# Bias as a ninth summand of the logits, a tile's factors in a tile of their own, and the next slot's gathers and scaling ahead of the scatters

## The chip, the cores and the metric

The kernel runs on one core of a Trainium2 chip. The metric is the device time of one execution in microseconds (us), the median over runs. TensorE is the matmul engine, VectorE (DVE) and ScalarE (ACT) the two engines that also read matmul results out of PSUM, GpSimd (POOL) the fourth, which here also issues the indirect DMAs; SyncE (SP) issues the other DMAs.

## What is computed

Attention over keys and values that are averaged over groups of 8 positions, then a mixture of experts in which each token goes to the one expert with the largest logit. Sizes: q, k, v are 8 x 8 x 576 x 64; 4608 tokens of width 512; 8 experts with a hidden width of 1024; 2 modalities.

```python
k_p = k.reshape(B, H, Sp, 8, D).mean(axis=3)            # v_p likewise
scores = scale * q @ k_p^T;  scores -= max;  attn = exp(scores) / (sum + 1e-9)
x = (attn @ v_p) as [4608, 512]
logits = x @ w_gate + modality_bias[modality_id]
e_idx = argmax(logits);  gate_w = softmax(logits)[e_idx]
out[tokens of e] = gate_w * (relu(x @ w1[e]) @ w2[e])
```

## The kernel before

**Attention.** 36 tiles of 128 tokens, in 20 steps (`steps`, L462); a step holds one or two tiles (z = 0 and 1), and a step with one tile mixes two batches. The loop at L906 works on a step in pieces that follow the engines' names: `s_pe`/`s_dve`/`s_act` make scores, subtract their maximum (`mx` L540, `sb` L543) and exponentiate; `t_pe`/`t_act` transpose the result (`pt`, L567); `a_pe` (L583) multiplies it by the values into one PSUM accumulator `av`, of which there is a single buffer. The values carry two more column groups: each head's product with the gate weights, and a column of ones, so that `av` also holds each head's eight logit shares and its sum. Pooling of k and v for the next batches runs on POOL (`fold`, L302 to L306), hooked into certain steps; in step 5 a hook also builds `bias_all`, the modality bias of all tokens, on POOL (`modality_terms`, L446).

**`x_dve(t)` (L603)** takes a tile out of `av`: DVE forms the sums (`s8`, L620), their reciprocals `r` (L622), and multiplies the logit shares by them into `lgs[g]` (L624), a tile for the nine token tiles of a group. For tiles with `late` (groups 2 and 3, z = 1; eight of them) the reciprocal is written into the row buffer `xw` itself, at its columns RX, and ACT copies the unscaled output beside it (L627); those rows are scaled after they are gathered again. For the others DVE multiplies the output by the factors (L630, `xb`). Rows go to the DRAM buffer `xs` by SP.

**`route(g)` (L661)** is a list of small DVE operations: reduction over the 8 heads (L679), bias add (L680), maximum over experts (L681), difference and exponential (L684, ACT L685), mask of the largest (L688), and so on. For groups 0 to 2 the list goes into `drip`; `gap(n)` takes up to n operations off its head at fixed places between the operations of `s_dve` and `x_dve`. Of the list of group 3, seven operations are issued at the end of the attention (L983) and the others, by their numbers in the list, inside the first expert slots (L1102).

**Experts.** Tokens sorted by expert are worked in slots of 256 rows (`part(s)`, L1124; 18 slots in this data, `NSTAT` = 18). Weights are split in two float32r halves by ACT and DVE; a slot is 8 times 12 matmuls `hp` (L170) and 6 matmuls `op` (L1160), and the 8 transposes (L161) of the next slot's rows. In a slot s, at f = 0, the previous slot's result is scaled by the gates (`evac`, L1131: DVE L1136, ACT L1138) and scattered by two indirect DMAs (L1142); then POOL gathers the next slot's rows with two indirect DMAs (L1204 by way of L143), scales them by the factors at f = 3 (L1219 by way of L152), and TensorE transposes them at f = 5. `evac(later=...)` puts the scatters into a list that is emptied behind the scaling; before, only slot 1 uses it. All engines execute their instructions in program order; the order above is written out by hand.

Of the kernel before, what the change touches and what calls it, by code (L numbers as in the profile page):

```python
# [9 lines left out]
F32 = mybir.dt.float32  # L10
# [12 lines left out]
P = 128  # L23
SLOT = 256
EARLY_GROUPS = 2
EARLY_SLOTS = 2
# [4 lines left out]
def kernel(  # L31
# [12 lines left out]
    nc = tc.nc  # L44
    ctx.enter_context(tc.manual_schedule(engines=ENGINES))
    B, H, S, HD = q.shape
    NTOK, D = out.shape
    E, _, FF = w1.shape
# [9 lines left out]
    RX = D + 8  # L58
    NSTAT = NTOK // SLOT
    NSLOT = (NTOK + EARLY_SLOTS * SLOT - 1 - E) // SLOT + E  # L60
    NCOL = 2 * NSLOT
    GT = 9
    GROUPS = [(GT * i, GT) for i in range(B // 2)]
# [127 lines left out]
    with ExitStack() as actx:  # L191
        ap = actx.enter_context(tc.tile_pool(name="ap", bufs=1))
# [207 lines left out]
        bias_all = ap.tile([P, NT, E], F32, name="bias_all")  # L400
# [182 lines left out]
        def a_pe(t):  # L583
# [9 lines left out]
            for u in range(2):  # L593
# [6 lines left out]
                for hs, y in halves:  # L600
                    nc.tensor.matmul(dst4[hs], pt4[:, hs], v4[y][:, 2 * u:2 * u + 2, :], start=False, stop=True)  # L601

        def x_dve(t):  # L603
            n, z = tile_step[t]
            g, gi = tile_group[t]
            av = avs.pop(t)
            mixed = steps[n][1] is None
            b = steps[n][0]
            if gi == 0:
                lgs[g] = late_p.tile([P, GT, H, E], F32, tag="lg", bufs=2, name=f"lg_{g}")  # L610
            xw = xbs[n if n < NX0 else NX0 + n % (len(xbs) - NX0)]
            xo = xw[:, z, 0:D]
            avv = av[:, :, 0:4 * VC].rearrange("p u (h x) -> p u h x", h=4)
            s8 = ap.tile([P, 2, 4], F32, tag="r", bufs=4, name=f"r_{t}")


            late = g >= EARLY_GROUPS and z == 1
            r = xw[:, z, RX:RX + H].rearrange("p (u h) -> p u h", u=2) if late else s8
            rb = r.rearrange("p u (h o) -> p u h o", o=1)
            nc.vector.tensor_scalar(s8, avv[:, :, :, VC - 1], float(POOL), 1e-9 * POOL, op0=ALU.mult, op1=ALU.add)  # L620
            gap(1)
            nc.vector.reciprocal(r, s8)  # L622
            gap(1)
            nc.vector.tensor_tensor(lgs[g][:, gi].rearrange("p (u h) e -> p u h e", u=2), avv[:, :, :, HD:HD + E],  # L624
                                    rb.to_broadcast([P, 2, 4, E]), op=ALU.mult)
            if late:
                nc.scalar.copy(xo.rearrange("p (u h d) -> p u h d", u=2, h=4), avv[:, :, :, 0:HD])  # L627
            else:
                for u in range(2):
                    nc.vector.tensor_tensor(xo[:, u * D // 2:(u + 1) * D // 2].rearrange("p (h d) -> p h d", h=4),  # L630
                                            avv[:, u, :, 0:HD], rb[:, u].to_broadcast([P, 4, HD]), op=ALU.mult)
            gap(2)

            if mixed:
                for y in range(2):
                    r0 = (b - 1 + y) * S + 512
                    stores.append(lambda y=y, r0=r0: nc.sync.dma_start(xs[r0:r0 + 64, :], xw[64 * y:64 * y + 64, 0, :]))
            elif z == 1:
                jj = steps[n][1]
                stores.append(lambda: nc.sync.dma_start(  # L640
                    xs[b * S:b * S + 512, :].rearrange("(p j) x -> p j x", j=4)[:, 2 * jj:2 * jj + 2, :], xw))
# [19 lines left out]
        def route(g):  # L661

            t0, n = GROUPS[g]
            sl = slice(t0, t0 + n)
            lg = small("lgr", g, [P, n, E])
            ex = small("ex", g, [P, n, E])
            m1 = small("m1", g, [P, n])
            m2 = small("m2", g, [P, n])
            sm = small("sm", g, [P, n])
            dc = small("dc", g, [P, E])  # L670
            rs = small("rs", g, [P, n, E])
            rk = small("rk", g, [P, n])
            rki = small("rki", g, [P, n], I32)
            rkm = small("rkm", g, [P, n], I32)
            rkf = small("rkf", g, [P, n])
            V = nc.vector
            ops = []
            add = ops.append
            add(lambda: V.reduce_sum(lg, lgs[g].rearrange("p t h e -> p t e h"), axis=AX.X))  # L679
            add(lambda: V.tensor_add(lg, lg, bias_all[:, sl, :]))  # L680
            add(lambda: V.reduce_max(m1, lg, axis=AX.X))  # L681

            def sub():
                V.tensor_tensor(lg, lg, per_e(m1, n), op=ALU.subtract)  # L684
                nc.scalar.activation(ex, lg, AF.Exp)  # L685
            add(sub)

            add(lambda: V.scalar_tensor_tensor(lg, lg, 0.0, per_t(w8, n), op0=ALU.is_equal, op1=ALU.mult))  # L688
            add(lambda: V.reduce_max(m2, lg, axis=AX.X))
            add(lambda: V.tensor_tensor(oh[:, sl, :], per_t(w8, n), per_e(m2, n), op=ALU.is_equal))  # L690

            def pe():
                if g == len(GROUPS) - 1:
                    pr = ps_tr.tile([P, n, E], F32, tag="tr", name=f"pr_{g}")
                else:
                    pr = corner(n * E).rearrange("p (t e) -> p t e", e=E)
                nc.tensor.matmul(pr, tri, oh[:, sl, :], start=True, stop=False)
                nc.tensor.matmul(pr, ones, cum[:, g:g + 1, :].to_broadcast([P, n, E]), start=False, stop=False)
                for i in range(n - 1):
                    m = n - 1 - i  # L700
                    nc.tensor.matmul(pr[:, i + 1:n, :], ones, oh[:, t0 + i:t0 + i + 1, :].to_broadcast([P, m, E]),
                                     start=False, stop=(i == n - 2))
                rts[g] = pr
                if g == 0:
                    rts["e0"] = corner(E, n * E)
                    nc.tensor.matmul(rts["e0"], sel0, oh[:, 0, :], start=True, stop=True)
            add(lambda: V.reduce_sum(sm, ex, axis=AX.X))
            add(lambda: V.tensor_scalar_add(sm, sm, 1e-9))
            add(lambda: V.reduce_sum(dc, oh[:, sl, :].rearrange("p t e -> p e t"), axis=AX.X))

            def gates():
                V.reciprocal(gate[:, sl], sm)
                for z in range(2):
                    b = 2 * g + z
                    nc.sync.dma_start(xs[b * S:b * S + 512, D:D + 1].rearrange("(p j) o -> p (j o)", j=4),
                                      gate[:, t0 + 5 * z:t0 + 5 * z + 4], allow_slow_non_contiguous=True)
                    nc.sync.dma_start(xs[b * S + 512:(b + 1) * S, D:D + 1],
                                      gate[64 * z:64 * z + 64, t0 + 4:t0 + 5], allow_slow_non_contiguous=True)
            add(gates)
            add(lambda: V.tensor_add(cum[:, g + 1, :], cum[:, g, :], dc))  # L720
            held.add(pe)
            add(pe)
            if g == 0:
                add(lambda: V.tensor_copy(e0oh, rts["e0"]))
            if g >= EARLY_GROUPS:
                add(lambda: V.tensor_tensor(rs, rts[g], per_t(adjv, n), op=ALU.add))
                add(lambda: V.tensor_mul(rs, rs, oh[:, sl, :]))
            else:
                add(lambda: V.tensor_tensor(rs, rts[g], oh[:, sl, :], op=ALU.mult))
            add(lambda: V.reduce_sum(rk, rs, axis=AX.X))  # L730
            add(lambda: V.tensor_copy(rki, rk))
            add(lambda: V.tensor_single_scalar(rkm, rki, 127, op=ALU.bitwise_and))
            add(lambda: V.tensor_single_scalar(rki, rki, 7, op=ALU.logical_shift_right))
            add(lambda: V.tensor_copy(rkf, rkm))
            add(lambda: V.tensor_copy(rh[:, sl], rki))
            for i in range(n):
                add(lambda i=i: V.tensor_scalar(arow[:, t0 + i, :], iota_b, rkf[:, i:i + 1], None, op0=ALU.is_equal))
            return ops
# [70 lines left out]
        def at(hook, n, *fns):  # L809
            hook.setdefault(n, []).extend(fns)  # L810
# [38 lines left out]
        for f in range(NF):  # L849
            at((hook_1, hook_2, hook_3)[(f + 1) % 3], N - 2 + (f + 1) // 3, lambda f=f: first0(f))  # L850

        at(hook_0, 5, modality_terms)

        load_gate()
        load_k(1)
# [124 lines left out]
            gap()  # L980
        loads(N + 1)
        last_route = route(len(GROUPS) - 1)
        for fn in last_route[:7]:  # L983
            fn()


# [110 lines left out]
    ]  # L1097


    lr, c4 = last_route, 2 * EARLY_SLOTS  # L1100
    first_cols = table(c4, c4 + 6)
    late = {  # L1102
        (0, 0): [lr[9], lr[7], lr[11], lr[8]],
# [20 lines left out]
    def part(s):  # L1124
# [68 lines left out]
        def run(fs, tail):  # L1193
            later = []
            for f in fs:
                if f:
                    hidden(f)
                if f == 0:
                    if s == 1:
                        tail(later=later)  # L1200
                    else:
                        tail()
                    if nxt and EARLY_SLOTS <= s < NSTAT - 1:
                        gather(s + 1, gidx, 2 * (s + 1), xg)  # L1204
# [130 lines left out]
```

## Time and profile before

| | |
|---|---|
| median of 3 runs | 625.12 us (623.38 to 627.63) |
| the profiled execution | 627.34 us, span 625.5 us |
| TensorE matmuls busy | 601.5 us (96% of the span) |
| DVE / ACT / POOL busy | 414.8 / 347.6 / 245.8 us |
| mean granted TensorE clock | 0.996 of full speed |
| last matmuls of the attention | about 187 us |

A busy TensorE is not one at its peak, since matmuls overlap and their ends are modelled; what counts for an edit is where TensorE waits, and for whom. Times in rows are from the start of the span.

### The profile page before, as it was taken

What the parts mean: (1) busy time and instruction counts of PE and PEld (TensorE: products, weight loads), DVE (VectorE), ACT (ScalarE), POOL (GpSimd) and SP (SyncE); (2) the same over time, 40 slices, a digit from 0 to 9 for tenths busy, and PEclk for the clock granted to TensorE, in tenths of its full rate; (3) what the DMA queues carried; (4) which work ended last, traced back from release to release, by engine and by line L of the source; (5) the groups of instructions that cost most, each with busy time, mean ns of one, the idle gap of its engine ahead of it and who ended that gap; (6) DMA issues with size and microseconds to landing.
All of it is one profiled execution on the core that took longest, in us unless ns stands there. A gap on an engine that the chain in (4) does not pass through costs nothing.

```text
span 625.5 us, 12457 instructions
## 1 busy us (share of the span) xinstructions
PE 601.5 (96%) x4223; PEld 545.5 (87%) x4223; DVE 414.8 (66%) x803; ACT 347.6 (56%) x657; POOL 245.8 (39%) x323
## 2 busy tenths in 40 slices
PE   4899999999999999999999999999999999999996
PEld 3689889888898998999999999999999899999995
DVE  4866798789957578675665665665665665666661
ACT  2667566788541455555555555555555555555551
POOL 5689978663000342422422413522522422422510
PEclk9999899999999999999999999999999999999999
DMA  8999969874202811201201452201205601201200
GB/s 244 287 313 311 357 186 369 279 232 124 86 36 70 271 70 33 69 29 43 70 28 42 130 190 89 67 33 37 70 34 172 202 23 36 69 30 40 70 35 21
DMA packets 63241, 76.58 MB, mean 122 GB/s; under 512 B 15423, under 2 KB 42047, under 8 KB 63168
## 3 DMA queue, kind: packets, MB, share of 16 engines
q1 hardware_dynamic: 57168, 55.98, 28.7%
q0 software_dynamic: 6000, 19.72, 9.7%
q8 instruction: 35, 0.57, 0.4%
q14 instruction: 38, 0.31, 0.2%
HBM read 119.40 MB, written 19.45 MB: 222 GB/s over the span
## 4 chain that ended last, share of the span: by engine, by line
PE 80%; DVE 7%; issue 4%; POOL 3%; DMA 3%; ACT 1%; SPq 0%; POOLq 0%; DVEq 0%; ACTq 0%
PE op L1160 31%; PE hp L170 30%; PE av L597 5%; PE sc L533 3%; PE xt L161 2%; PE av L601 2%; PE pq L508 2%; PE pp L562 2%; PE ph L170 1%; DMA out_dram<-ob,sidx 1%; DMA k<-in_k_dram 1%; DVE sb L543 1%; POOL v L304 1%; DVE mx L540 1%; DVE kp L309 1%
## 5 line engine op out<-in xcount | busy, mean ns | idle before, releaser
L136 ACT CAST hl<-raw 128x1024 fp32r<-128x1024 f32 x138 | 144.8, 1049 | 138.6 <-PE op L1160 137.6
L170 PE MATMUL hp<-xh,hl 128*128 128x256 f32 x1152 | 186.1, 284 | 0.0
L139 DVE TENSOR_TENSOR hl<-raw,hl 128x1024 fp32r<-128x1024 f32 x144 | 179.4, 1247 | 0.0
L170 PEld LDWEIGHTS hp<-xh,hl 128*128 128x128 f32 x1152 | 166.1, 189 | 10.5
L1160 PE MATMUL op<-hl,hh 128*128 128x512 f32 x554 | 173.5, 394 | 0.0
L174 DVE SCALAR_TENSOR_TENSOR hlo<-hp,hh 128x256 fp32r<-128x256 f32 x139 | 58.8, 423 | 132.3 <-ACT hh L172 132.3
L1142 POOL DMA_INDIRECT out_dram<-ob,sidx x36 | 50.4, 1400 | 226.4 <-DVE ob L1136 175.4
L1160 PE MATMUL op<-hl,hlo 128*128 128x512 f32 x277 | 108.4, 391 | 0.0
L1160 PEld LDWEIGHTS op<-hl,hh 128*128 128x128 f32 x554 | 94.8, 189 | 12.1
L170 PE MATMUL hp<-xl,hl 128*128 128x256 f32 x576 | 92.0, 282 | 0.0
L172 ACT ACTIVATE hh<-hp 128x256 fp32r<-128x256 f32 x139 | 53.4, 384 | 49.3 <-PE hp L170 48.9
L170 PEld LDWEIGHTS hp<-xl,hl 128*128 128x128 f32 x576 | 79.0, 190 | 0.0
L143 POOL DMA_INDIRECT xg<-xs,gidx x38 | 41.5, 1092 | 69.3 <-DMA raw<-in_moe_w_dram 53.8
L1160 PEld LDWEIGHTS op<-hl,hlo 128*128 128x128 f32 x277 | 52.0, 188 | 11.8
L152 POOL TENSOR_TENSOR xg<-xg 128x512 f32<-128x512 f32 x34 | 45.0, 1326 | 31.4 <-DMA xg<-xs,gidx 31.3
L597 PE MATMUL av<-vw,pt 128*128 128x146 f32 (+1 forms) x320 | 50.6, 297 | 1.9 <-ACT pt L567 1.1
L597 PEld LDWEIGHTS av<-vw,pt 128*128 128x128 f32 (+1 forms) x320 | 40.5, 183 | 4.1 <-ACT pt L567 2.2
L533 PE MATMUL sc<-kt,qt 128*128 128x144 f32 x256 | 38.5, 295 | 0.0
L533 PEld LDWEIGHTS sc<-kt,qt 128*128 128x128 f32 x256 | 34.8, 198 | 0.2
L540 DVE TENSOR_REDUCE mx<-sc 128x8 f32<-128x576 f32 (+1 forms) x40 | 27.7, 692 | 9.7 <-PE sc L533 8.1
L164 DVE TENSOR_TENSOR xl<-xt,xh 128x512 fp32r<-128x512 f32 x38 | 24.5, 684 | 14.4 <-ACT xh L163 14.4
L601 PE MATMUL av<-vw,pt 128*128 128x146 f32 (+1 forms) x160 | 31.3, 295 | 1.0 <-POOL vw L397 0.8
(234 smaller groups left out, 709.2 us busy)
## 6 DMA issues: line engine op xcount, KB each, us to landing
raw<-in_moe_w_dram SPq DMA_DIRECT2D x304, 256.0 KB
xs<-xb SPq DMA_DIRECT2D x16, 528.0 KB
k<-in_k_dram SPq DMA_DIRECT2D x7, 1024.0 KB
v<-in_v_dram SPq DMA_DIRECT2D x7, 1024.0 KB
q<-in_q_dram SPq DMA_DIRECT2D x6, 1024.0 KB
q<-in_q_dram SPq DMA_DIRECT2D x4, 512.0 KB
v<-in_v_dram SPq DMA_DIRECT2D x16, 128.0 KB
xs<-xb SPq DMA_DIRECT2D x8, 132.0 KB
```

The lines of the kernel that those rows point to most:

```text
L136: nc.scalar.copy(hl[f][:, 0, :], raw[f])
L139: eng.tensor_sub(hl[f][:, 1, :], raw[f], hl[f][:, 0, :].bitcast(F32))
L143: nc.gpsimd.indirect_dma_start(out=xgs[(2 * s + tt) % len(xgs)], out_offset=None, in_=xs[0:rows, :], in_offset=IndirectOffsetOnAxis(idx[:, ...
L152: nc.gpsimd.tensor_tensor(xv, xv, x[:, RX:RX + H].rearrange("p (h o) -> p h o", o=1).to_broadcast([P, H, HD]), op=ALU.mult)
L170: nc.tensor.matmul(ph, hl[f][:, w, d * P:(d + 1) * P], x[:, d, :], start=(n == 0 and d == 0), stop=(n == 2 and d == ND - 1))
L172: nc.scalar.activation(hh, ph, AF.Relu)
L174: nc.vector.scalar_tensor_tensor(hlo, ph, 0.0, hh.bitcast(F32), op0=ALU.max, op1=ALU.subtract)
L533: nc.tensor.matmul(dst, qt[:, i, :], kt[b % NB][:, :, h * SPL:(h + 1) * SPL], start=True, stop=True)
L597: nc.tensor.matmul(av[hs, u, 2 * VC * gg:2 * VC * (gg + 1)], pt[:, c, hs], vw[y][:, c].rearrange("p a x -> p (a x)"), start=(gg == 0), sto ...
L601: nc.tensor.matmul(dst4[hs], pt4[:, hs], v4[y][:, 2 * u:2 * u + 2, :], start=False, stop=True)
L1142: nc.gpsimd.indirect_dma_start(out=out[:, :], out_offset=IndirectOffsetOnAxis(idx.bitcast(U32), 0), in_=ob, in_offset=None, bounds_check=N ...
L1160: nc.tensor.matmul(o[tt], l[:, ts_], hl[f][:, w, D:2 * D], start=(f == 0 and n == 0), stop=(f == NF - 1 and n == 2))
```

## The change

Three edits and what follows from them.

- `lgs[g]` gets a ninth row beside the eight heads, and POOL copies the bias of the group's tiles into it (`bias_in`): for group 0 behind `modality_terms` in step 5, for the others at the first tile of the group. The reduction then runs over nine summands, and the add L680 is gone. The list of the last group is one shorter: six operations are issued at the end of the attention, and `[None] + last_route` keeps the numbers of the rest.
- `r` is always a tile of its own. For late tiles ACT copies it to the columns RX of the row buffer, behind its copy of the output.
- In slots 1 to `NSTAT - 2`, no longer in slot 1 alone, the scatters of the previous slot are held back until the next slot's gathers and scaling are issued.

```diff
--- before.py
+++ after.py
@@ -600,6 +600,11 @@
                 for hs, y in halves:
                     nc.tensor.matmul(dst4[hs], pt4[:, hs], v4[y][:, 2 * u:2 * u + 2, :], start=False, stop=True)
 
+        def bias_in(g):
+
+            t0, n = GROUPS[g]
+            nc.gpsimd.tensor_copy(lgs[g][:, :, H, :], bias_all[:, t0:t0 + n, :])
+
         def x_dve(t):
             n, z = tile_step[t]
             g, gi = tile_group[t]
@@ -607,7 +612,9 @@
             mixed = steps[n][1] is None
             b = steps[n][0]
             if gi == 0:
-                lgs[g] = late_p.tile([P, GT, H, E], F32, tag="lg", bufs=2, name=f"lg_{g}")
+                lgs[g] = late_p.tile([P, GT, H + 1, E], F32, tag="lg", bufs=2, name=f"lg_{g}")
+                if g:
+                    bias_in(g)
             xw = xbs[n if n < NX0 else NX0 + n % (len(xbs) - NX0)]
             xo = xw[:, z, 0:D]
             avv = av[:, :, 0:4 * VC].rearrange("p u (h x) -> p u h x", h=4)
@@ -615,16 +622,17 @@
 
 
             late = g >= EARLY_GROUPS and z == 1
-            r = xw[:, z, RX:RX + H].rearrange("p (u h) -> p u h", u=2) if late else s8
+            r = ap.tile([P, 2, 4], F32, tag="ri", bufs=4, name=f"ri_{t}")
             rb = r.rearrange("p u (h o) -> p u h o", o=1)
             nc.vector.tensor_scalar(s8, avv[:, :, :, VC - 1], float(POOL), 1e-9 * POOL, op0=ALU.mult, op1=ALU.add)
             gap(1)
             nc.vector.reciprocal(r, s8)
             gap(1)
-            nc.vector.tensor_tensor(lgs[g][:, gi].rearrange("p (u h) e -> p u h e", u=2), avv[:, :, :, HD:HD + E],
+            nc.vector.tensor_tensor(lgs[g][:, gi, 0:H].rearrange("p (u h) e -> p u h e", u=2), avv[:, :, :, HD:HD + E],
                                     rb.to_broadcast([P, 2, 4, E]), op=ALU.mult)
             if late:
                 nc.scalar.copy(xo.rearrange("p (u h d) -> p u h d", u=2, h=4), avv[:, :, :, 0:HD])
+                nc.scalar.copy(xw[:, z, RX:RX + H].rearrange("p (u h) -> p u h", u=2), r)
             else:
                 for u in range(2):
                     nc.vector.tensor_tensor(xo[:, u * D // 2:(u + 1) * D // 2].rearrange("p (h d) -> p h d", h=4),
@@ -677,7 +685,6 @@
             ops = []
             add = ops.append
             add(lambda: V.reduce_sum(lg, lgs[g].rearrange("p t h e -> p t e h"), axis=AX.X))
-            add(lambda: V.tensor_add(lg, lg, bias_all[:, sl, :]))
             add(lambda: V.reduce_max(m1, lg, axis=AX.X))
 
             def sub():
@@ -849,7 +856,7 @@
         for f in range(NF):
             at((hook_1, hook_2, hook_3)[(f + 1) % 3], N - 2 + (f + 1) // 3, lambda f=f: first0(f))
 
-        at(hook_0, 5, modality_terms)
+        at(hook_0, 5, modality_terms, lambda: bias_in(0))
 
         load_gate()
         load_k(1)
@@ -980,7 +987,7 @@
             gap()
         loads(N + 1)
         last_route = route(len(GROUPS) - 1)
-        for fn in last_route[:7]:
+        for fn in last_route[:6]:
             fn()
 
 
@@ -1097,7 +1104,7 @@
     ]
 
 
-    lr, c4 = last_route, 2 * EARLY_SLOTS
+    lr, c4 = [None] + last_route, 2 * EARLY_SLOTS
     first_cols = table(c4, c4 + 6)
     late = {
         (0, 0): [lr[9], lr[7], lr[11], lr[8]],
@@ -1196,7 +1203,8 @@
                 if f:
                     hidden(f)
                 if f == 0:
-                    if s == 1:
+
+                    if 0 < s < NSTAT - 1:
                         tail(later=later)
                     else:
                         tail()
```

## Rows read from the trace of the kernel before

**Rows 1.** Ten-microsecond windows: busy time (instructions) per engine, granted clock, DMA share, GB/s.

```profile
70.00:80.00 10.00, 9.50 (x66) 8.95 (x66) 7.84 (x28) 5.28 (x18) 9.29 (x17) 0.83 1.06 355
...
190.00:200.00 10.00, 10.00 (x63) 8.34 (x62) 7.57 (x37) 1.34 (x3) 0.00 (x0) 1.00 0.07 4
```

**Rows 2.** Waits of TensorE's weight loads, 420 to 590 us: total us, times, longest.

```profile
PEld xt L161 <- POOL xg L152: 0.2, 1, 0.2
```

**Rows 3.** Timeline of two expert slots (start, us, engine line; in brackets idle time before).

```profile
566.46 3.03 POOL L152 TENSOR_TENSOR xg<-xg 128x512 f32<-128x512 f32 x2 [1.84 <-DMA xg<-xs,gidx]
...
569.66 1.02 PEld L161 LDWEIGHTS xt<-ident,xg 128*128 128x128 f32 x8
...
580.63 1.77 POOL L1142 DMA_INDIRECT out_dram<-ob,sidx  x1 [11.15 <-DVE ob L1136]
...
585.27 1.23 POOL L1142 DMA_INDIRECT out_dram<-ob,sidx  x1 [2.87 <-PE op L1160]
```

**Rows 4.** Timeline of step 6, the bias add of group 0: DVE, TensorE, ACT, POOL.

```profile
65.61 1.20 DVE L679 TENSOR_REDUCE lgr<-lg 128x72 f32<-128x576 f32 x1
67.80 1.28 DVE L680 TENSOR_TENSOR lgr<-lgr,bias_all 128x72 f32<-128x72 f32 x1 [0.98 <-POOL bias_all L457]
69.00 0.74 DVE L543 TENSOR_TENSOR sb<-sc,mx 128x576 f32<-128x576 f32 x1
...
69.74 0.21 DVE L681 TENSOR_REDUCE m<-lgr 128x9 f32<-128x72 f32 x1
...
69.99 0.42 DVE L684 TENSOR_TENSOR lgr<-lgr,m 128x72 f32<-128x72 f32 x1
...
70.47 0.74 DVE L630 TENSOR_TENSOR xb<-av,r 128x256 f32<-128x256 f32 x2
71.13 0.50 DVE L688 SCALAR_TENSOR_TENSOR lgr<-lgr,w 128x72 f32<-128x72 f32 x1
...
69.80 0.63 PE L390 MATMUL sc<-wgb,vt 128*128 128x32 f32 x4 [0.86 <-DVE sb L543]
...
71.26 1.20 PE L597 MATMUL av<-vw,pt 128*128 128x146 f32 x4 [0.50 <-DVE xb L630]
...
70.45 0.26 ACT L685 ACTIVATE ex<-lgr 128x72 f32<-128x72 f32 x1 [2.50 <-DVE lgr L684]
...
66.97 0.80 POOL L457 TENSOR_TENSOR bias_all<-bias_all,sc 128x288 f32<-128x288 f32 x1
...
75.11 0.61 POOL L369 TENSOR_TENSOR vw<-vp,m 128x256 f32<-128x256 f32 x1
```

**Rows 5.** Timeline of step 11, behind the bias add of group 1.

```profile
109.55 0.74 DVE L630 TENSOR_TENSOR xb<-av,r 128x256 f32<-128x256 f32 x2
...
110.35 0.77 PE L597 MATMUL av<-vw,pt 128*128 128x146 f32 x4
```

**Rows 6.** Timeline of a late tile: logit multiply, ACT's two copies, the next matmuls.

```profile
113.16 0.21 DVE L624 TENSOR_TENSOR lg<-av,xb 128x64 f32<-128x64 f32 x1
...
113.47 0.59 ACT L627 COPY xb<-av 128x512 f32<-128x512 f32 x1 [1.82 <-PE sc L574]
113.95 0.59 ACT L567 COPY pt<-pp 128x512 f32<-128x512 f32 x1
...
114.59 0.77 PE L597 MATMUL av<-vw,pt 128*128 128x146 f32 x4 [0.70 <-ACT pt L567]
```

**Rows 7.** Timeline: ACT and DVE read one score tile in PSUM.

```profile
137.94 0.55 ACT L581 COPY pt<-sc 64x128 f32<-64x128 f32 x2
...
138.52 0.17 DVE L792 TENSOR_SCALAR adjv<-sc 128x8 f32<-128x8 f32 x1 [0.79 <-ACT pt L581]
```

**Rows 8.** Groups of instructions: busy us, mean ns of one, idle before.

```profile
L396 ACT COPY vg<-sc 128x32 f32<-128x32 f32 x7 | 1.3, 187 | 0.0
```

**Rows 9.** Timeline: ACT writes and DVE reads the two halves of xh.

```profile
571.04 1.07 ACT L163 CAST xh<-xt 128x512 fp32r<-128x512 f32 x2
...
571.65 1.29 DVE L164 TENSOR_TENSOR xl<-xt,xh 128x512 fp32r<-128x512 f32 x2 [0.96 <-ACT xh L163]
```

## Prediction

> **What bounds the kernel now.** I read the ten-microsecond windows first, because a share over the whole run mixes two stages. In the attention stage (to about 187 us) TensorE is busy for 8 to 10 of every 10 us, and it sometimes waits. One such stretch is the only one with a lower granted clock, 0.83; in the expert stage TensorE is busy for the whole of every window, at full clock; the row of 190 to 200 us stands for the 43 windows from 180 to 610 [rows 1]. The reader is to see from this that an edit in the expert stage can only pay where it removes a TensorE wait, however long GpSimd (POOL) stands there. I therefore asked next for the waits of TensorE's weight loads from 420 to 590 us. There is one: 0.2 us for the scaled tokens [rows 2].
>
> The timeline of that stage shows why it is so short. The two scatters of a slot start 4.64 us apart although the first is issued in 1.77 us; gathers and scaling come behind the second one in POOL's program. In the tightest slot read, scaling ends at 569.49 and the transposes that need it load at 569.66 [rows 3]. That is a slack of 0.17 us. The late work on POOL is real, but it is nearly all covered by matmuls.
>
> In the attention stage I went to the timelines of VectorE (DVE), ScalarE (ACT), POOL and TensorE around the two places that the diff touches: the bias add of group 0 [rows 4], the same point of group 1 [rows 5], and a late tile whose output is copied by ACT [rows 6].
>
> **The change part by part: the bias as a ninth summand.** Removed: four DVE adds, one for each group of nine tiles. Added: four POOL copies of 128x72, and one eighth more input to each reduction over heads. What matters is where these stand.
>
> Group 0. Now the reduction runs from 65.61 to 66.81. The add then waits 0.98 us for the bias, which POOL finishes at 66.97 + 0.80 = 67.77, and itself takes 1.28 us, so that the subtraction of the score maxima (sb) starts at 69.00. TensorE waits 0.86 us for sb, then 0.50 us for the attention accumulator to come free (xb, which ends at 70.47 + 0.74 = 71.21), and its matmuls start at 71.26 [rows 4]. After the change the reduction, too, is behind the bias, since the ninth summand is one of its inputs. POOL's copy is not in the trace: its price lies between 0 and the 0.80 us of the 128x288 add there, and I take 0.3 because 72 elements are nearer to the low end. The reduction can start at 68.07. At 1.20 x 9/8 = 1.35 us it ends at 69.42. The interleaved list pops two operations at this point, so the place of the add is taken by the maximum over experts (L681), whose successor started 69.99 - 69.74 = 0.25 us behind it. sb then starts at 69.67: 0.67 us later, or 0.37 with a free copy. With every operation of the list one place earlier, the mask (L688, 0.50 us, today behind xb) comes ahead of xb, and it overwrites what ACT's exponential reads (0.26 us), so it also waits for that; 0.25 goes back for the maximum. This is up to 0.50 + 0.26 - 0.25 = 0.51 more. Together xb and the matmuls behind it are 0.37 to 1.18 us later. I take the middle, 0.8, because the exponential can partly run beside the reciprocal. What is late next is the attention accumulator of the following tile, on TensorE.
>
> Group 1 has its bias long before, so only the shift of the list counts. xb ends at 109.55 + 0.74 = 110.29 and the next matmuls into the accumulator start at 110.35: no slack [rows 5]. By the 0.51 of group 0 xb would be up to 0.5 later. But TensorE stands still for 0.70 us four microseconds on, behind ACT [rows 6], and that takes some of it back. I take 0.3, between 0 and 0.5. Group 2 has no row here: I take 0, between 0 and the same 0.5, since the list can also fall at a place where TensorE leads. Group 3 is routed at the head of the expert stage, where TensorE has no idle time [rows 1], so it costs nothing; were that cover gone, the longer reduction would cost 1.35 - 1.20 = 0.15 us less what the add took. The adds removed save nothing where DVE is covered, for the same reason.
>
> **The factors in a tile of their own.** For early tiles and the first tile of a late step this only renames the destination of a reciprocal: 0. For the eight late tiles the reciprocal no longer writes the row buffer, and ACT gains a copy of 128x8 behind its copy of the output. Nothing of that shape is in the trace. The nearest ACT copy, 128x32, took 187 ns [rows 8]; fixed time is likely most of it, so I take 0.19, with 0 below. Queued behind it on ACT is the copy pt, and the next accumulator matmuls wait for pt: pt ends at 113.95 + 0.59 = 114.54, the matmuls start at 114.59 [rows 6]. Could ACT's output copy start earlier in exchange? It starts 0.10 us after the end of DVE's logit multiply (113.16 + 0.21 = 113.37), today. That multiply reads the factors from the row buffer that ACT writes, and both read the same PSUM tile. If the buffer is the cause, the wait goes; if the PSUM tile is, it stays. A DVE read of another PSUM tile (L792, 138.52) started right where ACT's reads of that tile ended (137.94 + 0.55 = 138.49), and nothing that ACT wrote there is its input [rows 7]. So readers of one PSUM tile follow one another in this program, and I take it that the wait stays. TensorE waits behind such a pt in a part of the eight cases, so the cost is between 0 and 8 x 0.19 = 1.5 us; I take 0.3.
>
> A page of the Trainium skill speaks to this, PSUM — Partial Sum Buffer, section "PSUM bank collisions raise a hardware error": two engines must be kept apart on one bank and quadrant, a ScalarE read against a VectorE read included. By that rule ACT's copy goes on waiting and the edit costs the 0.3; without it the edit would gain the 0.7 of the second rival below. The trace agrees as far as [rows 7] go.
>
> **Gathers and scaling ahead of the scatters.** For slots 2 to 16 both scatters are held back until the next slot's gathers and scaling are issued. The gathers are moved past two indirect DMAs of POOL's queue and past the second's wait for the first: 585.27 + 1.23 - 580.63 = 5.87 us [rows 3]. They still wait for both evacuations, which read the gates in the tiles that the gathers overwrite, so some 5 us is left. The slack of the transposes goes from 0.17 to about 5 us, and the 0.2 us wait of [rows 2] goes away. The scatters land later by a similar amount; nothing reads them, their buffers are two slots deep, and the last slot's tail is not held back. No instruction is added, SP's queue is not moved. I take -0.2, between -0.2 and 0 here; other executions may hold a little more.
>
> **The sum.** +0.8 + 0.3 + 0.3 - 0.2 = +1.2 us. On the profiled execution (627.34 us, span 625.5) this would be 628.5; that execution is 2.2 us above the median, 625.12, and I add the difference to the median: 626.3.
>
> **The rivals.** First, slower: POOL holds DVE up. If the new POOL copy into a group's logits had to finish before DVE may write the other columns of that tile, DVE's first logit multiply of group 1 would stand behind POOL's folds and the product at L369, which ends at 75.11 + 0.61 = 75.72 [rows 4]; that multiply comes ahead of xb, today at 70.47. That is 5.2 us. It decides from the point where POOL lags DVE at the head of a group. For groups 2 and 3 together I add half as much again, as POOL has less to do later, so 8 us (an estimate from that one row): 633. Against it: two halves of one interleaved tile are kept apart today. ACT's two copies xh take 1.07 us together; at the 0.59 of a copy of that size [rows 6] the second starts at about 571.5, before DVE starts at 571.65 to read the first half [rows 9]. I give it 6 in 100.
>
> Second, ACT is freed: the wait for the multiply was due to the factors in the row buffer. Then the 0.70 us of [rows 6] goes, instead of 0.3 added: +0.8 + 0.3 - 0.7 - 0.2 = +0.2, so 625.3. For it speaks that the multiply is the last reader of that buffer; against it [rows 7]. 25 in 100.
>
> Third, all of the bias edit is hidden, and the earlier scaling removes waits that other executions have more of: about -1, 624. For it speaks the slack of only 0.17 us; against it, a single such wait of 0.2. 12 in 100.
>
> Fourth, the pipeline gains over 1%: this needs 6.25 us, or 0.4 per reordered slot, of waits that the windows don't show. 3 in 100.
>
> **How the numbers follow.** The forecast, no measurable change with a small loss, has 54 in 100, and gives 626.3. Its bounds are 0.4 - 0.2 = +0.2 with every unknown at its least and 1.2 + 0.5 + 0.5 + 1.5 = +3.7 with every one at its worst: 625.3 to 628.8. The second and third rival reach down to 624. The three runs before lie 1.7 below to 2.5 above their median, so the range is 622.8 to 629.8; outside it are the first and fourth rival and some spread. About 1% (6.25 us) is what a measurement of this kernel can tell from no change. Slower by more: the first rival, 0.06. Faster by more: the fourth, 0.03. Same: 0.91.
>
> **What would show it.** In the changed profile: DVE's reduction of group 0 waiting about 2.2 us for POOL; TensorE's wait for sb at that place growing from 0.86 to about 1.5; a low clock there still. ACT's output copies starting 0.1 us after the logit multiply, and a small ACT copy behind each of the eight. Scaling ending some 5 us ahead of the transposes, with no such wait left, and expert slots of the same length. I am wrong if DVE waits for POOL at the first tile of a group, if ACT's output copy starts before the multiply ends, or if the slots get shorter.

## The result, and the profile after

The changed kernel takes 627.75 us (median of 16 runs, 625.49 to 630.38); the kernel before, beside it on the same chip, 625.80 us. The ratio is 1.0031 with a 95% interval of 1.0017 to 1.0046: slower by about 1.95 us (1.1 to 2.9). That is within the 1% that was forecast, and 1.5 us above the 626.3 predicted. Half of these 1.5 us is the base: the prediction started from 625.12 us, the median of three runs, and the sixteen runs give 625.80.

The profiled execution after has a span of 626.0 us. First the same windows as [rows 1] (busy time and instructions of TensorE (PE), its weight loads, DVE, ACT and POOL, then granted clock, DMA share, GB/s):

```profile
70.00:80.00 10.00, 9.49 (x58) 8.77 (x59) 6.63 (x24) 4.33 (x15) 9.29 (x18) 0.69 1.06 361
...
190.00:200.00 10.00, 10.00 (x62) 8.22 (x61) 7.45 (x33) 1.34 (x3) 0.00 (x0) 1.00 0.13 27
```

The expert stage is as full as before. The clock of the window that holds group 0 fell from 0.83 to 0.69, and fewer instructions fit into it (58 matmuls instead of 66).

Group 0, timeline of DVE, PE and POOL, which answers to [rows 4]:

```profile
66.36 1.34 DVE L687 TENSOR_REDUCE lgr<-lg 128x72 f32<-128x648 f32 x1 [2.39 <-POOL lg L606]
67.73 0.23 DVE L688 TENSOR_REDUCE m<-lgr 128x9 f32<-128x72 f32 x1
67.88 0.75 DVE L543 TENSOR_TENSOR sb<-sc,mx 128x576 f32<-128x576 f32 x1
...
69.30 0.35 DVE L695 SCALAR_TENSOR_TENSOR lgr<-lgr,w 128x72 f32<-128x72 f32 x1 [0.21 <-ACT ex L692]
...
69.71 0.74 DVE L638 TENSOR_TENSOR xb<-av,ri 128x256 f32<-128x256 f32 x2
...
68.68 0.63 PE L390 MATMUL sc<-wgb,vt 128*128 128x32 f32 x4 [1.46 <-DVE sb L543]
...
70.51 1.34 PE L597 MATMUL av<-vw,pt 128*128 128x146 f32 x4 [0.70 <-DVE xb L638]
...
72.13 1.18 PE L597 MATMUL av<-vw,pt 128*128 128x146 f32 x4
...
76.53 0.66 PE L597 MATMUL av<-vw,pt 128*128 128x146 f32 x4
...
65.23 0.79 POOL L457 TENSOR_TENSOR bias_all<-bias_all,sc 128x288 f32<-128x288 f32 x1
66.09 0.24 POOL L606 COPY lg<-bias_all 128x72 f32<-128x72 f32 x1
```

The wait for the bias has moved from the add to the reduction, as predicted, and grew from 0.98 to 2.39 us. PE's wait for sb grew from 0.86 to 1.46, that for xb from 0.50 to 0.70. Behind them four accumulator matmuls take 1.34 and 1.18 us; four of the same shape at full clock, at 76.53, took 0.66. The granted clock in windows of 2 us shows for how long. Before, 70 to 76 us:

```profile
70.00:72.00 2.00, 1.50 (x9) 1.35 (x9) 1.93 (x8) 1.55 (x5) 1.84 (x5) 0.86 1.05 291
72.00:74.00 2.00, 2.00 (x10) 2.00 (x10) 1.84 (x6) 0.57 (x4) 1.84 (x4) 0.50 1.07 395
74.00:76.00 2.00, 2.00 (x17) 1.59 (x17) 1.50 (x8) 0.78 (x2) 1.84 (x6) 0.79 1.02 377
```

After, 68 to 76 us:

```profile
68.00:70.00 2.00, 1.12 (x6) 0.95 (x6) 1.78 (x7) 0.99 (x4) 1.84 (x4) 0.84 1.06 326
70.00:72.00 2.00, 1.49 (x6) 1.50 (x7) 1.93 (x7) 1.12 (x6) 1.76 (x5) 0.50 1.04 386
72.00:74.00 2.00, 2.00 (x10) 1.99 (x9) 0.89 (x6) 0.00 (x0) 1.84 (x5) 0.50 1.04 396
74.00:76.00 2.00, 2.00 (x13) 1.28 (x12) 1.44 (x6) 1.05 (x3) 1.92 (x5) 0.50 1.09 362
```

0.50 is the lower of the two levels (1.2 GHz). Taking the share of each window that this needs, the engine ran (0.28 + 1 + 0.42) x 2 = 3.4 us at that level before and, with 0.96 in the window from 76 to 78 us, (0.32 + 3 + 0.08) x 2 = 6.8 us after.

A late tile, which answers to [rows 6]:

```profile
112.96 0.22 DVE L631 TENSOR_TENSOR lg<-av,ri 128x64 f32<-128x64 f32 x1
113.28 0.59 ACT L634 COPY xb<-av 128x512 f32<-128x512 f32 x1 [2.02 <-DVE lg L631]
...
113.76 0.20 ACT L635 COPY xb<-ri 128x8 f32<-128x8 f32 x1
113.86 0.59 ACT L567 COPY pt<-pp 128x512 f32<-128x512 f32 x1
...
114.50 0.77 PE L597 MATMUL av<-vw,pt 128*128 128x146 f32 x4 [0.33 <-ACT pt L567]
```

The output copy still starts 0.10 us behind the multiply's end, although that multiply no longer reads anything that ACT writes. The small copy lasts 0.20 us, and pt starts 0.10 us after the small copy's start.

An expert slot, which answers to [rows 3]:

```profile
563.18 1.04 POOL L152 TENSOR_TENSOR xg<-xg 128x512 f32<-128x512 f32 x1 [1.02 <-DMA xg<-xs,gidx]
564.38 2.01 POOL L1149 DMA_INDIRECT out_dram<-ob,sidx  x1 [0.16 <-issue]
568.40 1.00 POOL L1149 DMA_INDIRECT out_dram<-ob,sidx  x1 [2.01 <-DMA out_dram<-ob,sidx]
570.08 1.02 PEld L161 LDWEIGHTS xt<-ident,xg 128*128 128x128 f32 x8
```

Scaling now ends at 564.22, 5.9 us ahead of the transposes, where 0.17 us was left. The second scatter waits 2.01 us for the first to land. The wait of [rows 2] is gone; that the new order took it away is not shown, since two of the experiments below, whose scatters are as before, lack it too.

**Where the time went.** All the kernels here issue the same 4,223 matmuls in one order, so the start of each can be subtracted from that of the same one before. In us, at the matmul that ran at the given time before (the difference at 50 us is the start-up, which in these executions is 0.4 to 3.3 us shorter than in that of before; the last three columns are what each stretch added):

```
kernel                      at 50  at 77  at 166  at 615 | group 0  late tiles  experts
changed                     -1.72  +0.23   +0.58   +0.42 |   +1.95       +0.35    -0.16
ninth summand alone         -3.30  -1.36   -1.75   -1.91 |   +1.94       -0.39    -0.16
factor tile alone           -1.44  -2.47   -1.72   -1.89 |   -1.03       +0.75    -0.17
scatters held back alone    -0.42  -0.49   -0.51   -0.64 |   -0.07       -0.02    -0.13
late start of the list      -2.82  -4.09   -3.18   -3.34 |   -1.27       +0.91    -0.16
ACT copy first              -1.87  -2.85   -3.96   -3.83 |   -0.98       -1.11    +0.13
bias early, on ACT          -1.62  -4.98   -4.99   -5.03 |   -3.36       -0.01    -0.04
changed, bias early         -1.56  -3.46   -3.37   -3.53 |   -1.90       +0.09    -0.16
bias early, ACT copy first  -0.51  -3.58   -4.67   -4.68 |   -3.07       -1.09    -0.01
bias on ACT in step 5       -0.65  +3.15   +3.16   +3.00 |   +3.80       +0.01    -0.16
changed, the same           -2.01  +1.82   +1.88   +1.70 |   +3.83       +0.06    -0.18
```

The experiments below are the rows behind the first; "bias early" is the table made in step 4. Each row is a single execution. The changed kernel lost 1.95 us at group 0 and 0.35 between group 0 and the end of attention.

### The profile page after: what moved, and what is told of

Same layout as the page of the kernel before. It is cut to its first block, busy times and chain, and to the rows that moved or that the text cites. A ratio compares the mean times of both kernels' runs of the same rounds, so it can differ in the third digit from the quotient of the medians.

```text
span 626.0 us, 12436 instructions
## 1 busy us (share of the span) xinstructions
PE 601.6 (96%) x4223; PEld 545.3 (87%) x4223; DVE 416.6 (67%) x799; ACT 348.2 (56%) x665; POOL 258.2 (41%) x327
## 4 chain that ended last, share of the span: by engine, by line
PE 67%; issue 4%; DMA 2%; DVE 1%; POOL 0%; POOLq 0%; ACT 0%; DVEq 0%
PE op L1167 31%; PE hp L170 30%; PE xt L161 2%; PE ph L170 1%; DMA out_dram<-ob,sidx 1%; PE av L597 1%; DMA xg<-xs,gidx 1%; PE ptab L1057 0%; DVE hl L139 0%; POOL xg L152 0%; PE av L601 0%; PE pp L562 0%; DVE mx L540 0%; DVE xl L164 0%; POOLq L1338 0%
## 5 line engine op out<-in xcount | busy, mean ns | idle before, releaser
L139 DVE TENSOR_TENSOR hl<-raw,hl 128x1024 fp32r<-128x1024 f32 x144 | 183.5, 1276 | 0.0
L143 POOL DMA_INDIRECT xg<-xs,gidx x38 | 55.4, 1457 | 223.1 <-DVE ob L1143 147.3
L597 PE MATMUL av<-vw,pt 128*128 128x146 f32 (+1 forms) x320 | 50.4, 297 | 1.9 <-DVE xb L638 0.9
L152 POOL TENSOR_TENSOR xg<-xg 128x512 f32<-128x512 f32 x34 | 40.8, 1200 | 26.7 <-DMA xg<-xs,gidx 26.5
L567 ACT COPY pt<-pp 128x512 f32<-128x512 f32 x36 | 21.1, 586 | 19.0 <-PE pp L562 18.7
```

The costliest lines, as they stand in the source:

```text
L139: eng.tensor_sub(hl[f][:, 1, :], raw[f], hl[f][:, 0, :].bitcast(F32))
L143: nc.gpsimd.indirect_dma_start(out=xgs[(2 * s + tt) % len(xgs)], out_offset=None, in_=xs[0:rows, :], in_offset=IndirectOffsetOnAxis(idx[:, ...
L152: nc.gpsimd.tensor_tensor(xv, xv, x[:, RX:RX + H].rearrange("p (h o) -> p h o", o=1).to_broadcast([P, H, HD]), op=ALU.mult)
L597: nc.tensor.matmul(av[hs, u, 2 * VC * gg:2 * VC * (gg + 1)], pt[:, c, hs], vw[y][:, c].rearrange("p a x -> p (a x)"), start=(gg == 0), sto ...
```

## The experiments

**One part at a time.** The three parts were put alone into the kernel before: the ninth summand (`lgs` with H + 1, `bias_in`, no add), the factor tile (`r = ap.tile(... tag="ri")` and the small copy), the held-back scatters (`if 0 < s < NSTAT - 1`).

> Only the ninth summand (no tile of factors, scatters as before). Theory: most of the 1.95 us sits here, at the bias of group 0: TensorE waits 1.4 to 1.5 us there instead of 0.86, and the stretch at the lower clock behind it is longer by about 1 us; ratio about 1.002 to 1.003, +1.2 to +1.9 us. Rival, the cost lies in the factor tile or in the scatters: ratio 1.000 and TensorE's matmuls at that place no later than before.

> Only the tile of factors with ACT's eight extra copies. Theory: ACT's output copy starts 0.08 to 0.10 us after the logit multiply in all eight cases, as before, although no one reads the row buffer any more, and TensorE loses 0.1 to 0.2 us at three or four of them: +0.3 to +0.6 us, ratio 1.0005 to 1.001. Rival, the wait came from the factors in the row buffer: the copy starts right after the attention matmuls and the 0.70 us wait of TensorE goes, ratio 0.999.

> Only the order of gathers, scaling and scatters. Theory: scaling ends 4 to 6 us ahead of the transposes, the slots keep their 23.4 us, nothing moves: ratio 1.000 (0.999 to 1.001). Rival, scaling beside other DVE work or gathers beside weight loads cost something: expert slots longer by 0.05 us or more each, ratio 1.001 or above.

Measured, as ratios to the kernel before: ninth summand 1.0022 [1.0001, 1.0043], factor tile 1.0015 [0.9991, 1.0039], scatters 1.0006 [0.9985, 1.0027]. The times alone give only the first as a loss; the table gives places. The ninth summand alone repeats the loss at group 0 (+1.94), with nearly the same waits and the same slow matmuls:

```profile
64.83 1.34 DVE L686 TENSOR_REDUCE lgr<-lg 128x72 f32<-128x648 f32 x1 [2.28 <-POOL lg L606]
...
67.15 0.63 PE L390 MATMUL sc<-wgb,vt 128*128 128x32 f32 x4 [1.31 <-DVE sb L543]
...
68.98 1.34 PE L597 MATMUL av<-vw,pt 128*128 128x146 f32 x4 [0.63 <-DVE xb L637]
```

The factor tile loses 0.75 at the late tiles and nothing elsewhere. Its -1.03 at group 0 comes from its execution: no low clock followed there, with the same two waits as before (0.85 and 0.50). One of its windows:

```profile
70.00:72.00 2.00, 2.00 (x18) 1.83 (x19) 1.93 (x8) 1.11 (x6) 1.76 (x5) 1.00 1.03 370
```

The kernel with ACT's copy first, below, whose instructions at group 0 are those of before, shows the same: waits of 0.90 and 0.50 us, a clock of 1.00 in every window of 2 us from 62 to 80 us, and -0.98 in the table. The scatters alone, again with the code of before at group 0, had the 3.4 us of low clock and -0.07 (with a wait of 0.72 us for q in place of the one for sb). So the low clock behind these waits comes in some executions of the same code and not in others. Matmul by matmul, both executions without it gain 1.67 us over the stretch that was slow before, and give back 0.66 at the next accumulator matmuls, where PE now waits 0.42 us for xb. The 3.4 us were thus worth 1.67 us, of which 1.0 stayed.

The scatters move nothing. The -0.16 of the expert stage is in the rows of the ninth summand alone and of the factor tile alone too, where no scatter was touched, so it is not theirs; these two executions also lack the wait of [rows 2].

**Starting the list later.** In the changed kernel, group 0's list starts in the third hook of its step, when the bias has long been made:

```
-            at(hook_0, n, start)
+            at(hook_2 if g == 0 else hook_0, n, start)
```

> The changed kernel with one edit: the routing list of group 0 is started later in the same step (behind the second half's scores), when the bias has long been there. Theory, the wait for the bias and the lower clock behind it are the cost: no DVE wait for POOL at group 0, TensorE's two waits there and the low clock gone, ratio 0.994 to 0.997 against the kernel before, since before had 0.86 + 0.50 us of waits and about 2 us of slow matmuls there too. Rival, the clock falls for another reason: the low stretch stays, ratio 0.998 to 1.002.

Measured: 1.0021 [0.9997, 1.0045], so the expectation missed. DVE waited for no POOL instruction there, and the clock stayed at 1.00, but a new wait took the place (ACT and PE rows):

```profile
71.24 0.26 ACT L692 ACTIVATE ex<-lgr 128x72 f32<-128x72 f32 x1 [3.79 <-DVE lgr L691]
71.41 0.57 ACT L567 COPY pt<-pp 128x512 f32<-128x512 f32 x1
...
72.03 0.77 PE L597 MATMUL av<-vw,pt 128*128 128x146 f32 x4 [1.70 <-ACT pt L567]
```

ACT's exponential of the list stands ahead of pt in ACT's program, and DVE comes to the list only behind PE's next accumulator. The wait was moved from DVE to ACT's queue. The -1.27 at group 0 in the table is that of an execution without the low clock (the fastest of its twelve runs), to be set beside the -1.03 and -0.98 above.

**Making the bias earlier.** Here the bias table is made on ACT (bias 0 plus modality times the difference), in step 5, first in the kernel before and then in the changed one:

```
+            nc.vector.tensor_sub(md, mb[:, 1, :], mb[:, 0, :])
+            nc.vector.tensor_copy(mf, mod[:, :, 0])
+            for e in range(E):
+                nc.scalar.activation(bias_all[:, :, e], mf, AF.Identity, bias=mb[:, 0, e:e + 1], scale=md[:, e:e + 1])
```

> The kernel before with the bias of all tokens made by ACT (eight small activations, with two small DVE operations ahead of them) in place of POOL's six operations, 3.3 us of POOL's queue. Theory, the bias comes late only because it stands in POOL's queue: the add of group 0 no longer waits, TensorE's waits of 0.86 and 0.50 us and the low clock at that place go, and the folds behind come 3 us earlier: -2.5 to -4.5 us, ratio 0.993 to 0.996. Rival, POOL's backlog or ACT takes the place of the wait: TensorE waits for pt or for pooled values instead, ratio 0.998 to 1.001.

> The changed kernel with the same edit. Theory, the ninth summand costs only through the late bias of group 0: its excess over the kernel before falls from +1.95 to what the factor tile costs, so it comes out within 0.8 us of the run with the terms alone: ratio to before 0.994 to 0.998. Rival, the ninth summand costs elsewhere as well (shifted list, POOL's copies): 1.5 us or more above the run with the terms alone.

Measured: 1.0068 [1.0049, 1.0087] and 1.0062 [1.0041, 1.0083]. The gain of the first missed: at group 0 the add stood behind no wait, but the edit had put a larger one at its own place (DVE, ACT and PE rows of the first):

```profile
56.95 1.39 DVE L450 TENSOR_TENSOR md<-mb 128x8 f32<-128x8 f32 x1
...
58.27 0.17 DVE L451 CAST mf<-mod 128x36 f32<-128x36 int32 x1
...
58.47 2.60 ACT L453 ACTIVATE bias_all<-mf,mb,md 128x36 f32<-128x36 f32 x8 [3.91 <-DVE mf L451]
...
60.95 0.56 ACT L560 COPY pt<-pp 128x512 f32<-128x512 f32 x1
...
61.56 1.34 PE L590 MATMUL av<-vw,pt 128*128 128x146 f32 x4 [4.03 <-ACT pt L560]
```

DVE reached the two operands late, ACT's eight activations waited for them, and pt stood behind those. The pair still tells something: with the same early table, the changed kernel is no slower than the kernel before (629.26 against 629.80), where the late table put them 1.95 us apart.

**Making it earlier without a stall.** POOL makes the two operands at the head of step 4, and the activations go, four and four, to the two places of that step where ACT idled (1.4 and 1.6 us):

```
...
+        hook_0.setdefault(4, []).insert(0, modality_start)
+        at(hook_1, 4, lambda: modality_terms(range(0, 4)))
+        at(hook_3, 4, lambda: modality_terms(range(4, E)))
```

> The kernel before, with the bias terms taken off POOL's backlog, where they ended at 67.77 us while DVE's add stood waiting: POOL makes two small operands at the start of step 4 (0.2 and 0.22 us), and ScalarE makes the table in eight activations of about 0.32 us, four where it idled for 1.4 us (from 50.3 us) and four where it idled for 1.6 us (from 55.0 us). Theory (group 0 loses by the late table, and by the lower clock behind that wait): DVE's add of group 0 waits for nothing, PE's wait for sb behind it goes, no stretch at the lower clock follows there, and the time falls by 1 to 3 us: ratio 0.995 to 0.998. Rival (the wait was hidden, or another of the same size stands behind it, as in the run with the start of the list moved): 0.998 to 1.002. Rival (ScalarE's eight activations delay pt, as they did when they stood at step 5): above 1.003, with a PE wait for pt between 50 and 58 us.

> The changed kernel with the bias table made in the same way and at the same places. Theory (the ninth summand costs only because the table of group 0 comes late): POOL's copy of the summand stands ready before the reduction, and this kernel and the kernel before with the same table differ by no more than 0.6 us (0.1%), against the 1.95 us (0.31%) between them with the late table; the rest is ScalarE's small copies of the factors. Rival (the longer reduction and POOL's copies cost time in every group, or the factor copies do): the two stay 1.5 to 2 us apart.

Measured: 0.9963 [0.9945, 0.9981] in the kernel before, 0.9947 [0.9928, 0.9965] in the changed one (623.32 and 623.00 us): both expectations held. Group 0 in the first of the two (DVE, then PE):

```profile
63.99 1.21 DVE L674 TENSOR_REDUCE lgr<-lg 128x72 f32<-128x576 f32 x1
65.24 0.23 DVE L675 TENSOR_TENSOR lgr<-lgr,bias_all 128x72 f32<-128x72 f32 x1
65.39 0.75 DVE L538 TENSOR_TENSOR sb<-sc,mx 128x576 f32<-128x576 f32 x1
...
67.16 0.53 PE L390 MATMUL sc<-wgb,vt 128*128 128x32 f32 x4
...
67.95 0.77 PE L592 MATMUL av<-vw,pt 128*128 128x146 f32 x4
```

None of these instructions waits, the clock is 1.00 in every window of 2 us from 62 to 80 us, and the add takes 0.23 us where it took 1.28 in [rows 4]. The whole stretch is 3.36 us shorter. Matmul by matmul, 1.69 of it is gained by the first accumulator matmul behind xb (the two waits of [rows 4] are 0.86 + 0.50 = 1.36 of that), and the other 1.67 over the stretch that was slow before; no new wait takes any of it back. With the ninth summand on top the times are not to be told apart (runs from 622.10 to 626.90 us without it, 622.22 to 623.94 with it).

One cost of the ninth summand does show in the profile of the changed kernel with the early bias. The mask, one place earlier in the list, stands ahead of xb and waits for ACT's exponential, and PE waits for xb (DVE, then PE):

```profile
67.57 0.76 DVE L690 SCALAR_TENSOR_TENSOR lgr<-lgr,w 128x72 f32<-128x72 f32 x1 [0.21 <-ACT ex L687]
...
69.19 0.77 PE L592 MATMUL av<-vw,pt 128*128 128x146 f32 x4 [0.62 <-DVE xb L633]
```

The changed kernel with the bias on ACT in step 5 has the same wait, 0.47 us (in its row it is made up for by a wait for pt at step 5 of 3.47 us instead of 4.03); neither kernel without the ninth summand has it. In the table this execution is 1.47 us behind the other at group 0: 0.49 were lost before 54 us, 0.69 at this wait, and 0.29 at the next accumulator matmuls. What the ninth summand cost in time was thus mainly the late bias. The longer reduction and POOL's copy cost PE nothing there (the matmuls behind sb keep the same distance of 0.49 us); the shifted list costs about half a microsecond in these two executions, which is less than the timed runs can tell.

**ACT's copy ahead of DVE's reads.** If readers of one PSUM tile follow one another in program order, the order can be turned round. In the kernel before, ACT's output copy of a late tile is issued ahead of DVE's first read of the accumulator:

```
+            if late:
+                nc.scalar.copy(xo.rearrange("p (u h d) -> p u h d", u=2, h=4), avv[:, :, :, 0:HD])
             nc.vector.tensor_scalar(s8, avv[:, :, :, VC - 1], float(POOL), 1e-9 * POOL, op0=ALU.mult, op1=ALU.add)
...
-            if late:
-                nc.scalar.copy(xo.rearrange("p (u h d) -> p u h d", u=2, h=4), avv[:, :, :, 0:HD])
-            else:
+            if not late:
```

> The kernel before with ACT's output copy of the eight late tiles put ahead of DVE's three reads in the program; DVE goes on writing the factors into the row buffer. Theory, readers of one PSUM tile follow one another in program order: ACT's copy starts when the attention matmuls end or when ACT is free, and DVE's first read starts about 0.04 us after it ends, in all eight cases, though it shares nothing else with the copy but the row buffer's other columns. TensorE's waits for pt at these tiles shrink: ratio 0.998 to 1.000. Rival, the row buffer orders them: DVE's sums start beside ACT's copy.

> The kernel before with that table and with ScalarE's output copy of a late tile issued ahead of DVE's reads of the same PSUM tile. Theory (two separate gains, at group 0 and at the late tiles): 1 to 3 us from the first and about 1.2 us from the second, ratio 0.993 to 0.997, the fastest of all kernels here. Rival (both gains are absorbed by one later wait): no faster than the better of the two alone, 0.996 to 0.999.

Measured: 0.9981 [0.9963, 0.9998] alone, and 0.9930 [0.9910, 0.9951] with the early bias (622.08 us), by its median the fastest kernel here, ahead of both the kernel before and the changed one. One late tile of the first:

```profile
131.47 0.59 ACT L621 COPY xb<-av 128x512 f32<-128x512 f32 x1 [0.63 <-PE av L601]
131.96 0.59 ACT L567 COPY pt<-pp 128x512 f32<-128x512 f32 x1
132.09 0.17 DVE L622 TENSOR_SCALAR r<-av 128x8 f32<-128x8 f32 x1 [1.82 <-ACT xb L621]
```

DVE's read starts 0.03 us after ACT's copy ends, and so it does in each of the eight late tiles (0.03 or 0.04). The wait has changed sides with the program's order. The weight loads' waits for ACT's pt from 77 to 163 us, before (total, times, longest) and with the copy first:

```profile
PEld av L597 <- ACT pt L567: 1.8, 4, 0.9
PEld av L601 <- ACT pt L581: 0.8, 3, 0.3
```

```profile
PEld av L597 <- DVE xb L630: 1.2, 1, 1.2
...
PEld av L597 <- ACT pt L567: 0.6, 1, 0.6
```

Not all of it stays. At the matmul that ran at 153 us before, the copy first is at -5.78 us against -2.85 at 77, so 2.9 ahead; from there to 166 us it gives back 1.8. PE now waits for DVE there, for xb (0.93 us), for a logit multiply (0.43) and for the last group's list (0.42). The two gains, at group 0 and at the late tiles, add up in the row of both edits (-3.07 and -1.09).

## Why the prediction was right, and by which steps it was not

The time fell into the range, the forecast case (a small loss that is under 1%) came, and every sign listed under what would show it was seen. The terms of the sum fared less well: +0.8, +0.3, 0, +0.3 and -0.2 were taken, and +1.95, about -0.4, 0, +0.75 and 0 were measured. That the sum still came near is in part luck.

**Group 0, +0.8 taken, +1.95 measured.** The mechanism was right in each of its links: POOL's copy 0.24 us (0.3 taken), the reduction 1.34 (1.35), sb directly behind the maximum, the mask ahead of xb. In PE's program they are worth +0.60 at the matmuls behind sb and +0.36 more at those behind xb, which makes 0.96 and lies within the 0.37 to 1.18 given. The step that failed is one the sum didn't have. The low clock of that window was read ([rows 1], 0.83) and expected to stay, but its length was taken as fixed. It went from 3.4 to 6.8 us, and that is the other 1.0 us. Matmul by matmul the difference stays near 1.10 while both executions are slow, and grows to 1.95 over the slow matmuls that only the changed kernel has. That the longer waits bring on the longer low stretch is suggested, not shown: both executions with the ninth summand and the late bias have 6.8 us, but of the four whose group 0 has the list of before two have 3.4 us and two, with the same waits, none. The timed runs point the same way without settling it. The mean clock of a run has a median of 0.996 over 68 runs of the kernel before, 0.993 over 16 of the changed kernel and 0.998 over 11 with the early bias; but this mean also holds the microseconds behind the last matmul, where the clock was low for 1.1 us in the profile before and for 3.7 us in the one after, at no cost. What decides it in a single execution stays open.

**Group 1, +0.3 taken, about -0.4 measured** (ninth summand alone, between 108 and 120 us). xb was hardly late: from the start of the reduction to xb it took 3.16 us before and 3.21 in that run. The mask did come ahead of it (0.35 us, behind a wait of 0.21), but the difference took 0.22 us where it had taken 0.70, and the add was gone. With the mask out of the way behind xb, the late tile's logit multiply came 3.14 us behind xb's start instead of 3.61, ACT's copy with it, and the 0.70 us of [rows 6] became 0.25. The prediction named this wait as what takes some of the loss back. With hardly a loss at xb, what it gave back (0.45 us) is the whole of the -0.4. Group 2 was 0 as taken (-1.76 and -1.75 at 120 and 153 us).

**The factor tile, +0.3 taken, +0.75 measured.** That the wait stays was right: the copy starts 0.08 to 0.10 us behind the multiply's end in seven of eight late tiles after, as in eight of eight before, and with the order turned round DVE waits for ACT instead. The rival by which ACT is freed falls with that. The Trainium skill says the same (PSUM — Partial Sum Buffer, "PSUM bank collisions raise a hardware error": a ScalarE read is kept apart from a VectorE read of the same bank and quadrant), and the runs agree in both orders. The size was off. A small copy pushes pt back by 0.10 us, not 0.19, but the weight loads wait for pt more often than the matmul rows showed: 1.8 + 0.8 us in seven waits before, 2.9 + 1.3 us in ten with the factor tile alone.

**The scatters, -0.2 taken, 0 measured.** The slack grew to 5.9 us (about 5 expected), and there was nothing to gain: the one wait of 0.2 us is missing in two executions with the old order as well.

**The other rivals.** POOL's copy for group 1 ran at 74.22 us and no DVE instruction waited for it; from 50 us on, POOL held DVE up nowhere but at group 0's reduction. The third rival hid the whole bias edit, and group 0 shows that it wasn't hidden. The gain over 1% needed waits that were not there. The sum that was measured, 1.95 - 0.4 + 0 + 0.75 + 0 = 2.3 us, is within the interval of the timed loss (1.1 to 2.9). Measured less taken, the terms differ by +1.15, -0.7, 0, +0.45 and +0.2, which makes +1.1: the error of group 1 offset part of the others, and the range of 7 us would have held any of these sums.

## What to carry to other kernels

An operand that comes late should be made earlier before it is folded into an earlier instruction; the fold alone moves the wait up the list and takes everything behind it along. Where a stretch already shows a lower granted clock, a longer wait there may have to be priced twice, once for itself and once for the matmuls behind it (here 0.96 and 1.0 us), and a single profile doesn't say whether the low clock will come again. Where two engines read one PSUM tile, it can pay to issue first the one that the critical engine waits for (here 2.9 us in the profile, of which 1.1 stayed).

## What the runs showed of the hardware

- The same code at group 0, with waits of about 0.9 us for sb and 0.50 for xb, was followed by 3.4 us at the lower clock in one execution and by none in another; those 3.4 us cost 1.67 us, of which 0.66 came back at a later wait.
- A small DVE add or subtraction of two operands in SBUF that runs beside an operation of POOL can last until that one ends. The add of 128x72 took 1.28 us in [rows 4] and 0.74 in the fastest kernel, and a subtraction of 128x8 took 1.39 in step 5; each ran beside a fold of POOL and ended 0.02 to 0.09 us behind it. With the early bias alone the add started as a fold was ending and took 0.23.
- An ACT copy of 128x8 shows as 0.20 us, but the next ACT instruction starts 0.10 us after its start.
- Two indirect scatters into one tensor in HBM don't overlap in this program: the second was issued 4.02 us after the first, 2.01 us of it a wait for the first to land. Whether the chip or the program's own order asks for that wait is not shown.
